# One bfloat16 matmul with two columns for the sum of squares of each weight unit, in place of two float32 matmuls

## The chip, the core and the metric

The kernel runs on one core of one Trainium2 chip. The metric is the device time of one execution in microseconds (us). The program is built with a scheduler that sets the order of the instructions on every engine, so a small edit can move instructions far away from it.

## What is computed

Attention for 4 batches of 12 heads (448 tokens, head dimension 64, RMS-normalized q and k), and then two feed-forward layers on its output:

```python
scores = scale * np.matmul(q_n, k_n.transpose(0, 1, 3, 2))
attn = softmax(scores)
x = np.matmul(attn, v), heads merged        # 1792 x 768
g = x @ w_gate                              # 768 x 1536
x = (g * sigmoid(g)) * (x @ w_val) @ w_out  # 1536 x 768
h = x @ w_in                                # 768 x 2048
out = (h * np.cos(h)) @ w2_out              # 2048 x 768
```

The weights arrive as 64-bit floats.

## The kernel before

Large products run on TensorE (PE) in float16 pairs: a weight and an activation are each split into a high and a low part, and three matmuls of 448 columns (lines 1002 to 1004 of `mm_piece`, line 1015 of `mm_out`) give the product. A weight must be scaled by a power of two before it is split, and this power comes from the sum of its squares.

Weights come in pieces of 128 partitions by 768 numbers. A piece goes through a chain: `load64` (DMA on the queue of SP into a tile `raw`, line 821; three such tiles in turn), `conv64` (three VectorE operations, lines 841 to 843, 64-bit to float32 in a tile `w`), `squares` (ScalarE Square with a running sum over the free axis, line 861; its full output lands in the upper half of the same `raw` tile, so that `raw` is free for the next load only after the Square), `unit_scale` (line 868: a matmul of a tile `full` of ones by the sums, which adds them over the 128 partitions and hands the total to every partition), `pow2_scale` (four small VectorE operations, lines 848 to 853: floor, exponent, the inverse scale `winv`, the scale `wsc`), `split16` (ScalarE high part, line 873; VectorE low part, line 874).

A unit is the set of pieces that share a scale: two pieces for each of 6 gate units, 6 val units and 8 units of `w2_in` (20 units), one piece for each of the 16 units of `w2_out`. There are 56 pieces and 36 units. `unit_scale` issues one float32 matmul of one column per piece and adds the two of a unit in PSUM:

```python
for i, n in enumerate(q):
    nc.tensor.matmul(ps[:, :1], full, n[:, 0:1], start=(i == 0), stop=(i == len(q) - 1))
```

Its output takes one of the three PSUM banks `s`, which the attention scores use too. The sums sit in tiles `nm` of a ring of 8, which other small results share.

The stages in time: from 0 to about 99 us the attention of the first batch is prepared and started (q and k are loaded, normalized and split, and turned by transposing DMAs on SP's queue, line 614; ScalarE copies what they bring, line 623, VectorE too, lines 621 and 622, and the scores follow, line 634). From 99 to about 335 the gate and val weights go through the chain (12 units of two) between the scores of the next batch (lines 444 and 453) and the first feed-forward products. From 335 to 737 the remaining batches run with weights that are ready. From 737 to 1106 the last batch and then the product with `w2_in` run; the 8 units of `w2_in` and the 16 of `w2_out` go through the chain meanwhile (`pre_step`, `w_conv`, `w_scale`), and `fin_h` (lines 1134 to 1149) computes the cosine. From 1106 on the product with `w2_out` runs alone.

SP issues the DMAs in its program order; a DMA that waits for a buffer holds back those behind it. The other engines also run their rows in order.

Of the kernel before, what the change touches and what calls it, by code (L numbers as in the profile page):

```python
# [9 lines left out]
F32 = mybir.dt.float32  # L10
F32R = mybir.dt.float32r
F16 = mybir.dt.float16
BF16 = mybir.dt.bfloat16
I32 = mybir.dt.int32
AF = mybir.ActivationFunctionType
ALU = mybir.AluOpType
# [124 lines left out]
def kernel(ctx: ExitStack, tc, q, k, v, g_q, g_k, w_gate, w_val, w_out, w2_in, w2_out, out):  # L141
    nc = tc.nc
    B, H, S, D = q.shape
    P = 128
# [12 lines left out]
    const = ctx.enter_context(tc.tile_pool(name="const", bufs=1))  # L157
# [15 lines left out]
    nm_p = ctx.enter_context(tc.tile_pool(name="nm", bufs=8))  # L173
# [16 lines left out]
    def bank(pool, tag):  # L190
        return pool.tile([P, 512], F32, tag=tag, name=tag)
# [8 lines left out]
    fold = const.tile([P, HP], F32, name="fold")  # L200
    ones = const.tile([P, P], F32, name="ones")
    full = const.tile([P, P], F32, name="full")
    NU = 36
    winv = const.tile([P, NU], F32, name="winv")
    wsc = const.tile([P, NU], F32, name="wsc")
    vsc = const.tile([P, 2 * B], F32, name="vsc")
# [11 lines left out]
    def emit_consts(gtmp):  # L218
        nc.sync.dma_start(gk, g_k.partition_broadcast(P))
        nc.sync.dma_start(gtmp, g_q.partition_broadcast(P))  # L220
        nc.vector.memset(half, -0.5)
        nc.vector.memset(hpi, math.pi / 2)
        make_identity(nc, ident)
        for h in range(2):
            hs = slice(HP * h, HP * h + HP)
            nc.gpsimd.tensor_copy(fold[hs], ident[hs, hs])
        nc.gpsimd.memset(full, 1.0)
        nc.gpsimd.tensor_copy(id16, ident)
        nc.gpsimd.memset(ones, 0.0)
        for h in range(2):  # L230
            hs = slice(HP * h, HP * h + HP)
            nc.gpsimd.memset(ones[hs, hs], 1.0)
# [583 lines left out]
    sq_dst = [None]  # L816
# [28 lines left out]

    def pow2_scale(ps, inv, sc):
        n = nm_p.tile([P, 4], F32, tag="nm", name="nm")
        nc.vector.tensor_scalar(n[:, 0:1], ps, 1e-30, None, op0=ALU.max)
        nc.vector.tensor_scalar(
            n[:, 1:2].bitcast(I32), n[:, 0:1].bitcast(I32), 1, 0x7F800000, op0=ALU.logical_shift_right, op1=ALU.bitwise_and  # L850
        )
        nc.vector.tensor_scalar(inv, n[:, 1:2], 2.0 ** 49, None, op0=ALU.mult)
        nc.vector.reciprocal(sc, inv)
# [3 lines left out]

    def squares(u, w32):
        q = nrm_t.setdefault(u, [])
        n = nm_p.tile([P, 4], F32, tag="nm", name="nm")  # L860
        nc.scalar.activation(sq_dst[0], w32, AF.Square, accum_out=n[:, 0:1])
        q.append(n)

    def unit_scale(u):
        q = nrm_t.pop(u)
        ps = bank(ps_s, "s")
        for i, n in enumerate(q):
            nc.tensor.matmul(ps[:, :1], full, n[:, 0:1], start=(i == 0), stop=(i == len(q) - 1))
        pow2_scale(ps[:, :1], winv[:, u:u + 1], wsc[:, u:u + 1])

    def split16(u, w32):
        wp = wp_tile(F16)
# [34 lines left out]
    def w_conv(j):  # L907
        if j >= len(pieces) or not pieces[j]["fresh"] or pieces[j]["kind"] == "out2":
            return
        pc = pieces[j]  # L910
        w32_t[j] = conv64(raw_t.pop(j))
        if pc["kind"] != "out1":
            squares(unit_of(pc), w32_t[j])

    def w_scale(j):
        if j < len(pieces) and pieces[j]["fresh"] and pieces[j]["last"] and pieces[j]["kind"] in ("gate", "val", "h"):
            unit_scale(unit_of(pieces[j]))
# [45 lines left out]
    def pre_step(more=True):  # L963
        done = False
        if pre_split and (pre_split[0][0] == "out2" or len(pre_split) > 1):
            kind, c, k0, w32 = pre_split.pop(0)
            if kind == "h":
                for kind, c, k0, w32 in ((kind, c, k0, w32), pre_split.pop(0)):
                    stores.append((scr[kind, c, k0], split16(UNIT0[kind] + c, w32)))
            done = True  # L970
        if pre_scale and (pre_scale[0][0] == "out2" or len(pre_scale) > 1):
            kind, c, k0, w32 = pre_scale.pop(0)
            unit_scale(UNIT0[kind] + c)
            if kind == "h":
                pre_split.append((kind, c, k0, w32))
                pre_split.append(pre_scale.pop(0))
            done = True
        if pre_conv:
            kind, c, k0, rw = pre_conv.pop(0)
            w32 = conv64(rw)  # L980
            squares(UNIT0[kind] + c, w32)
            if kind == "out2":
                stores.append((o32[c // 2][:, c % 2 * 768:(c % 2 + 1) * 768], w32))
            pre_scale.append((kind, c, k0, w32))
            done = True
        if pre_load and more:
            kind, c, k0 = pre_load.pop(0)
            rw = load64(w2_out, c, 0, 1, 768) if kind == "out2" else load64(w2_in, k0, c, 3, 256)
            pre_conv.append((kind, c, k0, rw))
            done = True  # L990
        return done
# [74 lines left out]
    def y_scale(b):  # L1066
        n = nm_p.tile([P, 4], F32, tag="nm", name="nm")
        nc.vector.tensor_reduce(n[:, 0:1], ynrm[:, b * KX:(b + 1) * KX], axis=AX.X, op=ALU.add)
        ps = bank(ps_s, "s")
        nc.tensor.matmul(ps[:, :1], full, n[:, 0:1], start=True, stop=True)  # L1070
        pow2_scale(ps[:, :1], ysc[:, B + b:B + b + 1], ysc[:, b:b + 1])
        ts = nc.vector.tensor_scalar
        sy, yi = ysc[:, b:b + 1], ysc[:, B + b:B + b + 1]
        ts(yhi[:, b, 0:1], yi, 1.0 / TWO_PI, None, op0=ALU.mult)
        ts(yhi[:, b, 1:2], yi, -1.0, None, op0=ALU.mult)
        ts(yhs[:, b, 0:1], sy, -PI_HI, None, op0=ALU.mult)
        ts(yhs[:, b, 1:2], sy, -PI_LO, None, op0=ALU.mult)
# [97 lines left out]
    c_p = start_ctx.enter_context(tc.tile_pool(name="cp", bufs=1))  # L1175
    gtmp = start_ctx.enter_context(tc.tile_pool(name="gtmp", bufs=1)).tile([P, D], F32, name="gtmp")
    emit_consts(gtmp)
    for i in range(3):
        c_const(i)
# [26 lines left out]
    for b in range(B):  # L1206
        sched = {}
        if b + 1 < B:
# [3 lines left out]
            for n in range(nst):  # L1212
                u = min(u for u in range(per) if sum(wt[:u + 1]) * nst > n * sum(wt))
# [52 lines left out]
    for c in range(NH):  # L1266
        j0 = j
        j += 2
        for b in range(B):
            ps = [bank(ps_s, "s"), bank(ps_t, "t")] if nh % 3 == 2 else [bank(ps_m, "mm") for _ in range(2)]  # L1270
# [28 lines left out]
    while j < len(pieces):  # L1299
        ps = [None] * nt  # L1300
# [49 lines left out]
```

## Time and profile before

| | |
|---|---|
| median of 3 runs | 1346.54 us (1341.5 to 1349.18) |
| profiled execution, first to last instruction | 1339.1 us |
| around that span in the runs | 2.4 us (fastest run) to 10.1 us (slowest), 7.4 at the median |
| PE busy | 1191.8 us (89%) |
| VectorE (DVE) busy | 880.0 us (66%) |
| ScalarE (ACT) busy | 681.0 us (51%) |
| GpSimd (POOL) busy | 471.9 us (35%) |

The profile shows the profiled execution by its span; its own time as a run is not listed apart, so the three runs' times stand beside it. Busy shares are means over stages with different limits. A wait row says who waited for whom, the total, the number of times and the longest. A timeline row gives start, duration and, in brackets, the idle time before it and what ended it; where rows overlap, the step from one start to the next is the cost.

### The profile page before, as it was taken

Reading aid. Unit: us, or ns where it says so; the run is one execution under the profiler, and the core shown is the slowest. Engines: PE = TensorE matmul, PEld = TensorE weight load, DVE = VectorE, ACT = ScalarE, POOL = GpSimd, SP = SyncE. Lnnn points to the kernel's source line nnn. Section 1 sums busy time; section 2 is a strip of 40 time slices with the busy share of each in tenths; the row PEclk is TensorE's granted clock in tenths of the full one; section 3 lists DMA queues with packets and bytes.
Section 4 is the critical chain, followed back from the end, with each engine's and each line's share of the span. In section 5 each row is a group of like instructions: output and inputs, shape, how many; then the busy total and the mean of one; then the engine's idle time right before and its main releaser. Section 6 shows DMA issues by size and latency. Waiting matters only on the chain.

```text
span 1339.1 us, 18253 instructions
## 1 busy us (share of the span) xinstructions
PE 1191.8 (89%) x6454; PEld 673.1 (50%) x6454; DVE 880.0 (66%) x1556; ACT 681.0 (51%) x1318; POOL 471.9 (35%) x351
## 2 busy tenths in 40 slices
PE   0688787778799988999899998999999998999998
PEld 0233243334674434864447654865555544666665
DVE  6878978999967788647773299668778886200000
ACT  2567577776435556445565266457777776100000
POOL 8621325555733456533545113413233232000000
PEclk9889798888889989999999999999999998999999
DMA  7535559987999987788867688650112237433221
GB/s 241 143 86 144 175 148 238 253 211 217 256 310 283 234 159 158 196 245 190 189 138 181 226 274 318 232 187 0 48 48 70 73 130 228 166 96 101 59 89 42
DMA packets 255196, 227.03 MB, mean 170 GB/s; under 512 B 177280, under 2 KB 205952, under 8 KB 255104
## 3 DMA queue, kind: packets, MB, share of 16 engines
q1 hardware_dynamic: 255104, 225.86, 60.0%
q8 instruction: 50, 0.82, 0.2%
q14 instruction: 42, 0.34, 0.1%
HBM read 147.13 MB, written 38.77 MB: 139 GB/s over the span
## 4 chain that ended last, share of the span: by engine, by line
PE 36%; DVE 19%; ACT 9%; DMA 8%; issue 5%; POOL 1%; SPq 1%; ACTq 0%; DVEq 0%; POOLq 0%
PE mm L1015 7%; PE s L1015 7%; PE mm L1002 6%; PE mm L1004 5%; PE mm L1003 5%; DMA PT<-p 3%; DMA T<-h 3%; DVE w L842 2%; PE t L1015 2%; ACT tmp L1143 2%; ACT tmp L1142 2%; DVE tmp L1140 2%; DVE tmp L1141 2%; DVE w L841 2%; DVE w L843 1%
## 5 line engine op out<-in xcount | busy, mean ns | idle before, releaser
L1002 PE MATMUL mm<-xy,wp 128*128 128x448 f16 x840 | 302.7, 361 | 22.8 <-ACT wp L873 8.9
L1003 PE MATMUL mm<-xy,wp 128*128 128x448 f16 x840 | 302.7, 360 | 0.0
L1004 PE MATMUL mm<-xy,wp 128*128 128x448 f16 x840 | 298.7, 360 | 2.6 <-DVE wp L874 2.4
L1015 PEld LDWEIGHTS <-g 128*128 128x128 f16 x1344 | 132.4, 98 | 92.8 <-issue 7.1
L1002 PEld LDWEIGHTS <-wp 128*128 128x128 f16 x960 | 96.8, 101 | 119.3 <-issue 22.7
L1004 PEld LDWEIGHTS <-wp 128*128 128x128 f16 x960 | 94.5, 99 | 97.4 <-issue 7.7
L1003 PEld LDWEIGHTS <-wp 128*128 128x128 f16 x960 | 95.6, 100 | 93.5 <-issue 16.0
L496 POOL TENSOR_TENSOR p<-pr,p 128x448 f16<-128x448 f32 x72 | 89.9, 1253 | 139.5 <-ACT p L487 120.9
L1149 POOL TENSOR_TENSOR g<-tmp,g 128x448 f16<-128x448 f32 x64 | 71.4, 1127 | 175.7 <-ACT g L1148 175.7
L943 POOL TENSOR_TENSOR wp<-w,wp 128x768 fp32r<-128x768 f32 x48 | 95.7, 1997 | 79.7 <-ACT wp L942 54.9
L463 ACT ACTIVATE pr<-s,sm,esc 128x448 f32<-128x448 f32 x126 | 90.1, 717 | 62.7 <-DVE sm L457 57.3
L1002 PE MATMUL mm<-g,wp 128*128 128x448 f32 x288 | 108.8, 378 | 0.1
L1003 PE MATMUL mm<-g,wp 128*128 128x448 f32 x288 | 107.6, 374 | 0.0
L1004 PE MATMUL mm<-g,wp 128*128 128x448 f32 x288 | 106.8, 371 | 0.1
L1015 PE MATMUL mm<-wp,g 128*128 128x384 f16 x576 | 101.0, 330 | 3.8 <-DVE tmp L1144 3.8
L1050 POOL TENSOR_TENSOR g<-tmp,g 128x448 fp32r<-128x448 f32 x48 | 63.1, 1329 | 106.2 <-ACT g L1049 106.0
L1015 PE MATMUL s<-wp,g 128*128 128x384 f16 x576 | 100.3, 328 | 0.0
L453 DVE TENSOR_REDUCE sm<-s 128x1 f32<-128x448 f32 x126 | 75.4, 615 | 19.7 <-PE s L444 19.5
L487 ACT ACTIVATE p<-pr 128x448 f16<-128x448 f32 x126 | 70.0, 571 | 30.6 <-DMA PT<-p 29.8
L321 POOL TENSOR_TENSOR ri<-ss,half 128x14 f32<-128x14 f32 x24 | 65.1, 2716 | 46.5 <-DVE ss L319 39.9
L841 DVE TENSOR_SCALAR w<-raw 128x768 int32<-128x768 int32 x68 | 49.6, 739 | 47.9 <-POOL wp L943 21.1
L842 DVE SCALAR_TENSOR_TENSOR w<-raw,w 128x768 int32<-128x768 int32 x68 | 80.2, 1190 | 0.7
(182 smaller groups left out, 2146.6 us busy)
## 6 DMA issues: line engine op xcount, KB each, us to landing
raw<-in_moe_w_out_dram SPq DMA_DIRECT2D x28, 768.0 KB, 5.4
wp<-scr_gate SPq DMA_DIRECT2D x36, 384.0 KB, 4.7
wp<-scr_val SPq DMA_DIRECT2D x36, 384.0 KB, 4.5
w<-scr_out SPq DMA_DIRECT2D x36, 384.0 KB, 4.3
raw<-in_moe_w_in_dram SPq DMA_DIRECT2D x16, 768.0 KB, 5.0
raw<-in_moe_w_gate_dram SPq DMA_DIRECT2D x12, 768.0 KB, 5.4
raw<-in_moe_w_val_dram SPq DMA_DIRECT2D x12, 768.0 KB, 4.6
wp<-scr_out SPq DMA_DIRECT2D x24, 384.0 KB, 3.0
```

The source lines that it names most:

```text
L453: nc.vector.tensor_reduce(sm[:, 0, t:t + 1], slot[n][:, :S], axis=AX.X, op=ALU.max)
L463: nc.scalar.activation(e, slot.pop(n)[:, :S], AF.Exp, bias=sm[:, 1, t:t + 1], scale=esc, accum_out=sm[:, 2, t:t + 1],)
L487: nc.scalar.activation(hi, slot[n], AF.Copy)
L496: eng.tensor_sub(p16[:, t - t0, 1], slot.pop(n), p16[:, t - t0, 0])
L841: nc.vector.tensor_scalar(wi, hi, 3, 0x3FFFFFF8, op0=ALU.logical_shift_left, op1=ALU.bitwise_and)
L842: nc.vector.scalar_tensor_tensor(wi, hi, -0x40000000, wi, op0=ALU.bitwise_and, op1=ALU.bitwise_or)
L943: nc.gpsimd.tensor_sub(wl, w32, wh.bitcast(F32))
L1002: nc.tensor.matmul(ps[f][:, :S], wh[:, s], x[:, 0], start=(first and i == 0), stop=False)
L1003: nc.tensor.matmul(ps[f][:, :S], wh[:, s], x[:, 1], start=False, stop=False)
L1004: nc.tensor.matmul(ps[f][:, :S], wl[:, s], x[:, 0], start=False, stop=(last and i == n - 1))
L1015: nc.tensor.matmul(ps[:, :CO], x[:, a, p0:p0 + P], rhs, start=st, stop=sp)
L1149: nc.gpsimd.tensor_sub(x[:, 1], r, x[:, 0])
```

## The change

The ones are also kept as a bfloat16 tile `full16`. The running sums of a unit's pieces go to columns 0 and 1 of one tile `nu` (a ring of 6 of its own). One bfloat16 matmul takes the upper 16 bits of these float32 sums (a view with a step of two elements) as its two columns, or its one column for a unit of one piece. The two totals are then added on VectorE by one operation more. Line numbers after the edit are 2 to 8 higher.

```diff
+    full16 = const.tile([P, P], BF16, name="full16")
...
+        nc.gpsimd.memset(full16, 1.0)
...
     def pow2_scale(ps, inv, sc):
         n = nm_p.tile([P, 4], F32, tag="nm", name="nm")
-        nc.vector.tensor_scalar(n[:, 0:1], ps, 1e-30, None, op0=ALU.max)
+        if ps.shape[1] == 2:
+            nc.vector.tensor_scalar(n[:, 2:3], ps[:, 0:1], 1e-30, None, op0=ALU.max)
+            nc.vector.tensor_tensor(n[:, 0:1], ps[:, 1:2], n[:, 2:3], op=ALU.add)
+        else:
+            nc.vector.tensor_scalar(n[:, 0:1], ps, 1e-30, None, op0=ALU.max)
...
     def squares(u, w32):
         q = nrm_t.setdefault(u, [])
-        n = nm_p.tile([P, 4], F32, tag="nm", name="nm")
-        nc.scalar.activation(sq_dst[0], w32, AF.Square, accum_out=n[:, 0:1])
+        if not q:
+            q.append(nm_p.tile([P, 4], F32, tag="nu", name="nu", bufs=6))
+        n = q[0]
+        nc.scalar.activation(sq_dst[0], w32, AF.Square, accum_out=n[:, len(q) - 1:len(q)])
         q.append(n)
 
     def unit_scale(u):
         q = nrm_t.pop(u)
+        m = len(q) - 1
         ps = bank(ps_s, "s")
-        for i, n in enumerate(q):
-            nc.tensor.matmul(ps[:, :1], full, n[:, 0:1], start=(i == 0), stop=(i == len(q) - 1))
-        pow2_scale(ps[:, :1], winv[:, u:u + 1], wsc[:, u:u + 1])
+        nc.tensor.matmul(ps[:, :m], full16, q[0].bitcast(BF16)[:, 1:2 * m:2], start=True, stop=True)
+        pow2_scale(ps[:, :m], winv[:, u:u + 1], wsc[:, u:u + 1])
```

The scheduler places other instructions differently too. Three places follow.

**Start, queues of SP and ACT.** SP's queue before, from the load of the second gate piece on (`raw<-` loads a weight piece, `T<-h` is the transposing DMA of one pair of heads; what a row waits for is in brackets):

```order
L821 DMA raw<-in_moe_w_gate_dram 128x3x512 [waits DMAHW7_49,DMAHW5_49,DVE_49]
L821 DMA raw<-in_moe_w_val_dram 128x3x512 [waits DMAHW6_49,DMAHW0_49,DVE_49]
L614 DMA_TRANSPOSE T<-h_313 128x14x128 [waits Pool_49]
L281 DMA rqk<-in_k_dram 64x448
L281 DMA rqk<-in_k_dram 64x448 [waits DMAHW1_49]
L284 DMA rqk<-in_q_dram 128x448 [waits DMAHW2_49]
L614 DMA_TRANSPOSE T<-h_335 128x14x128 [waits DMAHW3_49,Pool_49]
```

SP's queue after the change, from the same load on:

```order
L823 DMA raw<-in_moe_w_gate_dram 128x3x512 [waits DMAHW7_49,DMAHW5_49,DVE_49]
L823 DMA raw<-in_moe_w_val_dram 128x3x512 [waits DMAHW6_49,DMAHW0_49,DVE_49]
L823 DMA raw<-in_moe_w_val_dram 128x3x512 [waits DMAHW1_49,Activation_49]
L616 DMA_TRANSPOSE T<-h_315 128x14x128 [waits Pool_49]
L283 DMA rqk<-in_k_dram 64x448
L283 DMA rqk<-in_k_dram 64x448 [waits DMAHW2_49]
L286 DMA rqk<-in_q_dram 128x448 [waits DMAHW3_49]
L616 DMA_TRANSPOSE T<-h_337 128x14x128 [waits DMAHW4_49,Pool_49]
```

ACT's queue at the same place before (`h` is the split q and k of a pair of heads, `cC` a copy of what its transposing DMA brought):

```order
L392 ACTIVATE h_313<-rqk 128x7x64
L392 ACTIVATE h_335<-rqk 128x7x64
L623 ACTIVATE cC<-T 64x896
L378 ACTIVATE h_384<-rqk 128x7x64
L392 ACTIVATE h_384<-rqk 128x7x64
```

and after the change:

```order
L394 ACTIVATE h_315<-rqk 128x7x64
L394 ACTIVATE h_337<-rqk 128x7x64
L869 ACTIVATE raw,nu<-w_738 128x768
L869 ACTIVATE raw,nu<-w_813 128x768
L869 ACTIVATE raw,nu<-w_887 128x768
L625 ACTIVATE cC<-T 64x896
L380 ACTIVATE h_386<-rqk 128x7x64
L394 ACTIVATE h_386<-rqk 128x7x64
```

The Squares of the first three pieces (line 869, 861 before) now stand ahead of the copy that waits for the first transposing DMA, and the load of the fourth piece, which waits for ACT (its `raw` tile is the first piece's), stands ahead of that DMA on SP.

**DVE, a val unit of two pieces in the stretch from 99 to 335 us.** Before, from the end of the conversion of the unit's second piece (`w_1782`) to the four small operations:

```order
L843 SCALAR_TENSOR_TENSOR w_1782<-raw,w_1782 128x768
L398 TENSOR_TENSOR h_2250<-rqk,h_2250 128x7x64
L843 SCALAR_TENSOR_TENSOR w_1858<-raw,w_1858 128x768
L384 TENSOR_TENSOR h_2250<-rqk,h_2250 128x7x64
L453 TENSOR_REDUCE sm<-s 128x1 x2
L848 TENSOR_SCALAR nm<-s 128x1
L849 TENSOR_SCALAR nm<-nm 128x1
L852 TENSOR_SCALAR winv<-nm 128x1
L853 RECIPROCAL wsc<-winv 128x1
L874 SCALAR_TENSOR_TENSOR wp<-w_1718,wsc,wp 128x768
```

and after the change, the same unit (`w_1779`):

```order
L845 SCALAR_TENSOR_TENSOR w_1779<-raw,w_1779 128x768
L845 SCALAR_TENSOR_TENSOR w_1854<-raw,w_1854 128x768
L851 TENSOR_SCALAR nm<-s 128x1
L1043 TENSOR_SCALAR nm<-winv,vsc 128x1
L852 TENSOR_TENSOR nm<-s,nm 128x1
L455 TENSOR_REDUCE sm<-s 128x1
L855 TENSOR_SCALAR nm<-nm 128x1
L455 TENSOR_REDUCE sm<-s 128x1
L1047 SCALAR_TENSOR_TENSOR tmp<-tmp,mm 128x448
L858 TENSOR_SCALAR winv<-nm 128x1
L455 TENSOR_REDUCE sm<-s 128x1
L1047 SCALAR_TENSOR_TENSOR tmp<-tmp,mm 128x448
```

One conversion of the next piece is all that now stands between the end of the unit's conversion and the first operation on its total (`L851`). The small operations, which stood together right ahead of the low part (line 874), now have maxima of scores and products of the gate between them; the reciprocal (line 859) is the next row.

**ACT, last units of one piece (`w2_out`), around 1065 to 1080 us.** Before, with the Squares of `w_10300` and `w_10377` behind the high parts (line 873) of the units before:

```order
L873 ACTIVATE wp<-w_10076,wsc 128x768
L873 ACTIVATE wp<-w_10126,wsc 128x768
L1143 ACTIVATE tmp<-tmp,hpi,ht 128x448
L1148 ACTIVATE g_10263<-tmp 128x448
L1134 ACTIVATE tmp<-mm,ht 128x448 x2
L861 ACTIVATE raw,nm<-w_10300 128x768
L1148 ACTIVATE g_10272<-tmp 128x448
L1142 ACTIVATE tmp<-tmp 128x448 x2
L1143 ACTIVATE tmp<-tmp,hpi,ht 128x448 x2
L1134 ACTIVATE tmp<-s,ht 128x448
L1134 ACTIVATE tmp<-t,ht 128x448
L861 ACTIVATE raw,nm<-w_10377 128x768
```

and after the change, where `w_10359` is the piece that was `w_10377`, and `w_10059`, `w_10109` are those that were `w_10076`, `w_10126`:

```order
L1142 ACTIVATE tmp<-mm,ht 128x448
L869 ACTIVATE raw,nu<-w_10359 128x768
L1156 ACTIVATE g_9972<-tmp 128x448
L1150 ACTIVATE tmp<-tmp 128x448
L1151 ACTIVATE tmp<-tmp,hpi,ht 128x448
L1150 ACTIVATE tmp<-tmp 128x448
L1151 ACTIVATE tmp<-tmp,hpi,ht 128x448
L881 ACTIVATE wp<-w_10059,wsc 128x768
L881 ACTIVATE wp<-w_10109,wsc 128x768
```

The Square of that piece moved from eleven rows behind the first of these high parts to six rows ahead of it. Those of its three neighbours moved likewise, while their matmuls on PE stand behind the same count of products as before.

## Rows read from the trace of the kernel before

**Rows 1.** Stretches of the span; columns: us, busy time of each engine (instructions), PEclk, DMA share, GB/s.

```profile
0.00:99.00 99.00, 48.68 (x189) 17.84 (x190) 76.16 (x141) 44.75 (x77) 58.61 (x59) 0.91 0.57 158
99.00:335.00 236.00, 185.29 (x914) 85.03 (x914) 206.00 (x330) 163.16 (x334) 99.67 (x69) 0.88 0.72 197
...
737.00:892.00 155.00, 150.60 (x795) 103.45 (x794) 105.91 (x205) 71.80 (x124) 43.26 (x26) 1.00 0.76 260
892.00:1106.00 214.00, 210.99 (x1127) 110.23 (x1126) 176.74 (x348) 160.41 (x281) 63.30 (x58) 1.00 0.19 62
```

**Rows 2.** PE timeline; start us, duration us, line, op, operands, xcount, then idle before it.

```profile
946.63 0.35 PE L1004 MATMUL t<-xy,wp 128*128 128x448 f16 x1
946.82 0.50 PE L868 MATMUL s<-nm,full 128*128 128x1 f32 x4
947.18 0.35 PE L1002 MATMUL mm<-xy,wp 128*128 128x448 f16 x1
```

**Rows 3.** PE timeline around a unit of one piece.

```profile
806.58 0.28 PE L868 MATMUL s<-nm,full 128*128 128x1 f32 x2
806.75 0.35 PE L1002 MATMUL mm<-xy,wp 128*128 128x448 f16 x1
```

**Rows 4.** Weight loads and matmuls of line 868 over the span; duration min/median/max.

```profile
L868 PEld LDWEIGHTS s<-nm,full x112: 186/190/338, 99.5 to 1096.4; 128*128 128x128 f32 x112
L868 PE MATMUL s<-nm,full x112: 165/250/373, 99.5 to 1096.5; 128*128 128x1 f32 x112
```

**Rows 5.** Weight loads of float16, from the costliest groups; xcount | busy us, mean ns.

```profile
L1002 PEld LDWEIGHTS <-wp 128*128 128x128 f16 x960 | 96.8, 101 | 119.3 <-issue 22.7
```

**Rows 6.** Waits of PE from 892 to 1106; us in total, times, longest.

```profile
PE s L868 <- ACT raw L861: 2.7, 3, 1.2
```

**Rows 7.** Waits of PE from 1106 on.

```profile
PE mm L1015 <- DVE tmp L1144: 3.8, 1, 3.8
```

**Rows 8.** Timeline of all engines where one unit of two pieces is finished.

```profile
312.11 1.81 DVE L843 SCALAR_TENSOR_TENSOR w<-raw,w 128x768 int32<-128x768 int32 x2
313.09 0.84 ACT L861 ACTIVATE raw<-w 128x768 f32<-128x768 f32 x1 [3.42 <-DVE w L843]
313.84 0.19 ACT L861 ACTIVATION_READ_ACCUMULATOR raw<-w 128x1 f32 x1
...
314.08 0.38 PE L868 MATMUL s<-nm,full 128*128 128x1 f32 x2 [2.29 <-ACT raw L861]
```

**Rows 9.** DVE timeline of small operations.

```profile
181.66 0.15 DVE L849 TENSOR_SCALAR nm<-nm 128x1 int32<-128x1 int32 x1
181.85 0.16 DVE L852 TENSOR_SCALAR winv<-nm 128x1 f32<-128x1 f32 x1
```

**Rows 10.** Waits of DVE from 99 to 335.

```profile
DVE wp L874 <- ACT wp L873: 7.4, 6, 2.0
...
DVE nm L848 <- PE s L868: 3.4, 2, 2.6
```

**Rows 11.** Waits of PE from 99 to 335.

```profile
PE s L868 <- ACT raw L861: 10.6, 4, 4.1
```

**Rows 12.** Timeline of the SP queue at the start.

```profile
28.29 2.58 SPq L614 DMA_TRANSPOSE T<-h  x1
...
57.20 0.38 SPq L821 DMA_DIRECT2D raw<-in_moe_w_val_dram  x1
```

**Rows 13.** Timeline of ACT at the start.

```profile
24.65 0.58 ACT L392 ACTIVATE h<-rqk 128x448 f16<-128x448 f32 x1 [1.31 <-POOL rqk L364]
33.73 0.95 ACT L623 ACTIVATE cC<-T 64x896 f16<-64x896 f16 x1 [8.50 <-DMA T<-h]
...
56.23 0.85 ACT L861 ACTIVATE raw<-w 128x768 f32<-128x768 f32 x1
```

**Rows 14.** Timeline of DVE at the start.

```profile
29.11 1.67 DVE L843 SCALAR_TENSOR_TENSOR w<-raw,w 128x768 int32<-128x768 int32 x1
...
34.73 0.39 DVE L621 COPY cB<-T 64x896 f16<-64x896 f16 x1
```

## The prediction

> **What bounds the kernel now.** I read the stretches of the span first, then the waits of the engine that is short in each, then single places in the timeline. From 737 us on PE is the bound: it is busy 150.6 of 155 us up to 892 and 211.0 of 214 up to 1106, at the full clock [rows 1]. What PE saves there shortens the run. From 99 to 335 no engine is full, but DVE is nearest, with 206 of 236 us busy against 185 for PE [rows 1]; an operation more on DVE counts nearly in full there, and matmul time counts little. Up to 99 us PE is busy half of the time [rows 1]: a chain of loads, splits and transposing DMAs sets the pace, and a delay in it delays all that follows.
>
> **What a unit costs on PE.** A float32 matmul of line 868 leaves two weight loads and two matmuls in the trace: 112 of each for 56 pieces, a load taking 190 ns [rows 4]. A unit of two pieces holds the stream for 947.18 - 946.82 = 0.36 us, where a product of 448 columns takes 0.19 [rows 2]. A unit of one piece holds it for 806.75 - 806.58 = 0.17 us [rows 3]. After the change a unit is one weight load and one matmul of one or two columns. No row shows a bfloat16 matmul so narrow. Its bounds are half of the one-piece unit, since half of the passes are left, 0.08 us, and a whole product of 448 columns, 0.19 us. I take 0.10, because such a short matmul should cost about its weight load, and 16-bit loads take 101 ns [rows 5]. That saves 0.26 us per unit of two pieces and 0.07 per unit of one.
>
> The Trainium skill ("FP8 and Floating Point Precision", section "TensorE Precision Notes") says that true FP32 takes four passes through the array. The trace shows two loads and two matmuls per operation, not four. By the rule a single pass would be 0.17/4 = 0.04 us, an estimate from that page, and the 24 units after 737 us would save some 1.4 us more than my sum has.
>
> **Part 1, from 737 us on.** There are 8 units of two pieces (of `w2_in`) and 16 of one (of `w2_out`): 8 x 0.26 + 16 x 0.07 = 3.2 us saved, all on the bound engine. With the two bounds of a unit this is between 1.0 and 4.1 us.
>
> PE also waits there for the Square of a piece: 2.7 us in three waits [rows 6]. The order after the change puts the last Squares of `w2_out` from eleven rows behind two high parts to six rows ahead of them, and leaves the matmuls at the same place in PE's stream. A row of ACT of 448 columns takes 0.58 us [rows 13], so the Squares come several us earlier than the matmuls need them, and I take all 2.7 as saved (none, if DVE's conversions ahead of the Squares are late instead). DVE, busy 177 of 214 us [rows 1], has room for one small operation more per unit, which costs nothing there; without that room the five units of two in this stretch would cost 1 us. Sum of part 1: 5.9 us saved, between 1.0 and 6.8. What follows at once is the product with `w2_out`; its first matmul that waits does so for the cosine chain on DVE, 3.8 us [rows 7]. That chain starts from PE's last products, so I let it move along with them.
>
> **Part 2, from 99 to 335 us.** Twelve units of two pieces pass here. Each has one DVE operation more. Small ones follow each other at 181.85 - 181.66 = 0.19 us [rows 9], so 12 x 0.19 = 2.3 us; DVE is busy 87% there, and I count 2.0 (bounds 0 and 2.3).
>
> The order changes more than that. The way from the end of a conversion through Square, its accumulator read and the matmul to the total is 314.08 + 0.38 - 313.09 = 1.4 us with nothing in the way [rows 8]. Before, in the unit shown, a conversion, two splits and two maxima of scores stood over it on DVE; after the change four val units have one conversion alone, 1.81/2 = 0.9 us [rows 8]. DVE then waits 0.5 us in each, 1.9 in all (0 if ACT and PE run ahead, 5.6 if no row covers it). PE's 10.6 us of waits for Squares [rows 11] remain in some form and are not on the bound.
>
> In return rows now stand between the reciprocal and the low part in units where none stood. DVE lost 7.4 us in six such waits for the high part, and 3.4 for totals [rows 10]. I count 4 of the 7.4 as recovered (0 to 7.4), since three of the twelve units had no cover before and every unit has some now. Part 2 is thus 2.0 + 1.9 - 4 = 0, with bounds of 7.4 saved and 7.9 lost.
>
> **Part 3, the start.** The load of the fourth weight piece needs the `raw` tile of the first, which its Square releases. Before, that Square ran at 56.23 [rows 13], and the load followed at 57.20, long after the first transposing DMA, issued at 28.29 [rows 12]. Now the load stands ahead of that DMA on SP, and SP must wait for the Square. The Square was moved up as well, but it cannot start before its conversion ends, 29.11 + 1.67 = 30.78 [rows 14]; ACT is free then, its row before ends at 25.23 [rows 13]. It takes 1.0 us [rows 8], and the issue of the load 0.38 [rows 12], so that the transposing DMA is issued at about 32.3, 4.0 us later. Queued behind it on SP are the loads of q and k of the next pairs and the second and third transposing DMAs. ACT's copy, at 33.73 before [rows 13], waits for what it brings, and with it the split of the third pair, which stands behind that copy; so the third is late by 4 too. DVE's copy at 34.73 [rows 14] slips to about 37.7, but a conversion of 0.9 us that stood behind it is done ahead now, so DVE waits from about 35.6 and loses some 2.0. Between 2.0 and 4.0 I take 3.0, because up to 99 us latency counts more than any engine's work; the lower end is 0, if slack behind it takes all. The new memset on POOL is one of several small ones ahead of work that waits for loads, and costs nothing; without that cover it is a fraction of a microsecond.
>
> **Sum.** 3.0 + 0 - 5.9 = 2.9 us saved against the span of 1339.1 us, so 1336.2. The median of the runs is 7.4 us above this span, so the time is 1343.6 us. That is 0.2% below the median; 0.5% (6.7 us) is about what a measurement of this kernel can tell from no change.
>
> **The rivals.** *A, the new order is better than its parts.* After the change the units of the second stretch come evenly, three scores apart. If DVE loses neither the 7.4 nor the 3.4 us [rows 10] and meets no new wait, and the start's slip is absorbed, the time is 1346.5 - 5.9 - 10.8 + 2.0 = 1331.8. For it: no unit is left without cover ahead of its low part. Against it: four units have less cover ahead of the total than any before.
>
> *B, SP's queue, the other side.* A load of weights that waits for a Square ahead of a transposing DMA costs 4.0 us at the start, and from about the fifteenth load on most loads stand one to three transposing DMAs earlier than before. Each that meets a late Square stops SP, and behind it the DMAs that feed the scores. With 5.9 us saved it takes 12.6 us, so the fourth such stop makes the run slower by over 0.5%; four give 1346.5 - 5.9 + 16 = 1356.6. For it: DMAs of the attention end waits of ACT in every stage. Against it: the Squares moved up too, and most loads are issued long before they are needed.
>
> *C, the saving is not passed on.* If the cosine chain [rows 7] does not move along, what PE saves after 892 us only lengthens its wait of 3.8, and about 1.6 us from before 892 is left: 1346.5 - 1.6 + 3.0 = 1347.9.
>
> *D, the change does not do what it says.* If the narrow matmul costs 0.19 us, the gain of 3.2 falls to 1.0 and the time is 1345.8.
>
> **How the numbers follow.** My forecast, with D beside it, 0.34, and C 0.10 lie within 0.5% (1339.8 to 1353.3): 0.44 for the same. A has 0.32, since the lost DVE and PE waits in the second stretch are larger than any cost that I can name. B has 0.24. The range reaches from A with the better bound of part 1 (1331.8 less 0.9, and 2 more should it also end some of PE's waits [rows 11]) to just past B: 1329 to 1358. It leaves out a fifth: the far ends of A and B.
>
> **What would show it.** Right: 36 weight loads in `unit_scale` instead of 112, near 100 ns each; steps near 0.1 us at the units after 737; no wait of PE for Squares from 892 to 1106; the first transposing DMA issued near 32.3; DVE waiting for the total in the val units. Wrong: that DMA still at 28; waits of DVE for high parts as long as before; the stretch from 99 to 335 shorter or longer by over 8 us; or a wait at the first products with `w2_out` that has grown by what PE saved.

## The result, and the profile after

The changed kernel takes 1357.88 us (median of 6 runs, 1352.97 to 1362.59) against 1344.72 for the kernel before in the same session: ratio 1.0099, 95% interval 1.0075 to 1.0122. It is slower by 1%, where 1343.6 was forecast. The time is inside the range, but the change was forecast to save 2.9 us and costs some 13.

First what was priced. PE's timeline at a unit of two pieces, which answers to [rows 2], and at a unit of one:

```profile
974.66 0.35 PE L1012 MATMUL t<-xy,wp 128*128 128x448 f16 x1
974.85 0.17 PE L876 MATMUL s<-nu,full 128*128 128x2 bf16 x1
974.88 0.35 PE L1010 MATMUL mm<-xy,wp 128*128 128x448 f16 x1
...
1090.75 0.17 PE L876 MATMUL s<-nu,full 128*128 128x1 bf16 x1
1090.78 0.35 PE L1010 MATMUL s<-xy,wp 128*128 128x448 f16 x1
```

The next product starts 0.03 us behind the sum in both, where it was 0.36 for two pieces and 0.17 for one. I had taken 0.10. The Trainium skill ("FP8 and Floating Point Precision", section "TensorE Precision Notes") has true FP32 take four passes; the estimate of 0.04 for a single pass that I worked out from that is nearer here than the 0.10 that I took from rows. The four passes themselves show in no run here. Line 876 over the span, for [rows 4], has 36 of each, a load of about 98 ns:

```profile
L876 PEld LDWEIGHTS <-full x36: 95/98/98, 98.2 to 1123.4; 128*128 128x128 bf16 x36
L876 PE MATMUL s<-nu,full x36: 163/167/178, 98.2 to 1123.6; 128*128 128x2 bf16 x20, 128*128 128x1 bf16 x16
```

SP's queue at the start, for [rows 12]: the first transposing DMA is issued at 32.36, where 32.3 was forecast. But by 98 us the slip is gone: the first sum of a unit runs at 98.2, where it ran at 99.5 [rows 4]. The traces of the experiments below say more: where the order of the start is the changed one, that sum runs at 95.5 to 97.8 (11 traces), and where it is that of before, at 100.5 to 102.2 (6). So by then the changed start is some 4 us ahead, not 3 behind.

```profile
26.11 6.19 SPq L823 DMA_DIRECT2D raw<-in_moe_w_val_dram  x2
32.36 2.83 SPq L616 DMA_TRANSPOSE T<-h  x1
```

Waits of DVE (first two) and of PE (last two) from 99 to 335 us, for [rows 10] and [rows 11]: DVE's wait for the high part fell from 7.4 to 3.2 us and its wait for totals from 3.4 to 2.3, as forecast, but PE waits 26.0 us for high parts, where it waited 8.9 before (second fence). Its wait for exponentials, 12.9 us before, is 0.9 now.

```profile
DVE wp L882 <- ACT wp L881: 3.2, 3, 1.5
DVE nm L851 <- PE s L876: 2.3, 4, 1.2
...
PE mm L1010 <- ACT wp L881: 26.0, 7, 7.3
PE s L876 <- ACT raw L869: 9.9, 6, 4.3
```

```profile
PE s L444 <- ACT pr L463: 12.9, 8, 4.6
...
PE mm L1002 <- ACT wp L873: 8.9, 6, 2.7
```

No engine is full there, and the stretch as a whole lost or gained little: its last unit's sum runs at 314.90 (PE's timeline), before at 314.08 [rows 8].

```profile
314.90 0.16 PE L876 MATMUL s<-nu,full 128*128 128x2 bf16 x1 [4.27 <-ACT raw L869]
```

From the first unit's sum to the last it takes 216.7 us, before 214.6; the other traces spread from 215 to 218 in the order of before and from 213 to 218 in the changed one, so no difference shows.

Laying PE's matmuls of the two traces side by side (by their count, the sums of the units left out), the changed kernel is 0 us behind at 413 us, 9 behind at 450, 14 at 700, 28 at 918, and 22 at the end. Of these 22 only 13 lie between the medians: the changed kernel's profiled execution was the longest of its six runs (1362.59), and the one before, with a span of 1339.1 us, is at the short end of its runs, so what is read off this pair can be too large by up to 9 us. Still, the time goes where the edited instructions are few or none, from 413 to 700, most of it by 450, and in the stretch before 918. That stretch by windows, for [rows 1] (busy time and instructions of PE, weight loads, DVE, ACT, POOL, then granted clock, DMA share, GB/s): the changed kernel, begun at 751 since it is 14 us behind there, then the kernel before:

```profile
751.00:919.00 168.00, 152.60 (x776) 100.80 (x775) 108.25 (x210) 72.28 (x127) 44.61 (x26) 0.97 0.73 246
```

```profile
737.00:905.00 168.00, 163.60 (x863) 110.17 (x862) 118.78 (x232) 81.61 (x137) 43.26 (x26) 1.00 0.72 246
```

In the same 168 us PE does 11 us less than before, DVE 11 and ACT 9; the DMAs move as much. So the three engines have come to wait, and PE is no longer full where my sum had it full. Its granted clock, 0.97 against 1.00, has dropped too.

The end of y at 905 to 918 is the largest single step. Timelines of ACT, DVE and PE of the changed kernel:

```profile
910.87 0.84 ACT L869 ACTIVATE raw<-w 128x768 f32<-128x768 f32 x1 [4.81 <-DVE winv L858]
914.68 0.84 ACT L869 ACTIVATE raw<-w 128x768 f32<-128x768 f32 x1 [2.87 <-DVE nm L855]
915.52 0.52 ACT L1065 ACTIVATE tmp<-mm 128x448 f32<-128x448 f32 x1
...
908.24 0.56 DVE L843 TENSOR_SCALAR w<-raw 128x768 int32<-128x768 int32 x1 [3.20 <-DMA raw<-in_moe_w_in_dram]
912.05 0.56 DVE L843 TENSOR_SCALAR w<-raw 128x768 int32<-128x768 int32 x1 [1.00 <-DMA raw<-in_moe_w_in_dram]
917.60 0.16 DVE L1076 TENSOR_REDUCE nm<-ynrm 128x1 f32<-128x6 f32 x1 [2.55 <-ACT mm L1066]
...
917.81 0.37 PE L1078 MATMUL s<-nm,full 128*128 128x1 f32 x1 [5.24 <-DVE nm L1076]
```

The last evictions of y (line 1065) stand on ACT behind Squares of `w2_in` pieces (line 869), those behind conversions on DVE (line 843), and those behind loads that have not landed. `y_scale` (line 1076) comes last, and PE waits 5.24 us for it. In the kernel before, only the first of these two conversions stands ahead of that reduction (line 1068), the second stands behind it, and PE does not wait:

```profile
887.98 0.57 DVE L841 TENSOR_SCALAR w<-raw 128x768 int32<-128x768 int32 x1 [2.10 <-DMA raw<-in_moe_w_in_dram]
...
890.71 0.14 DVE L1068 TENSOR_REDUCE nm<-ynrm 128x1 f32<-128x6 f32 x1
...
897.21 0.56 DVE L841 TENSOR_SCALAR w<-raw 128x768 int32<-128x768 int32 x1
```

### The profile page after: what moved, and what is told of

Read it like the earlier page. It is cut to its first block, busy times and chain, and to the rows that moved or that the text cites. A ratio compares the mean times of both kernels' runs of the same rounds, so it can differ in the third digit from the quotient of the medians.

```text
span 1360.8 us, 18117 instructions
## 1 busy us (share of the span) xinstructions
PE 1187.6 (87%) x6378; PEld 661.5 (49%) x6378; DVE 877.6 (64%) x1576; ACT 680.6 (50%) x1318; POOL 481.9 (35%) x352
## 4 chain that ended last, share of the span: by engine, by line
PE 35%; DVE 11%; DMA 7%; ACT 6%; issue 3%; POOL 1%; SPq 1%; ACTq 0%; DVEq 0%; POOLq 0%
PE mm L1023 7%; PE s L1023 6%; PE mm L1010 5%; PE mm L1011 5%; PE mm L1012 5%; PE t L1023 2%; DMA T<-h 2%; DVE w L844 2%; DMA PT<-p 1%; PE t L557 1%; ACT tmp L1150 1%; DVE tmp L1148 1%; DVE tmp L1149 1%; ACT tmp L1151 1%; DVE w L845 1%
## 5 line engine op out<-in xcount | busy, mean ns | idle before, releaser
L1157 POOL TENSOR_TENSOR g<-tmp,g 128x448 f16<-128x448 f32 x64 | 71.7, 1133 | 177.8 <-ACT g L1156 177.7
L1058 POOL TENSOR_TENSOR g<-tmp,g 128x448 fp32r<-128x448 f32 x48 | 67.0, 1411 | 121.5 <-ACT g L1057 121.2
L869 ACT ACTIVATE raw<-w 128x768 f32<-128x768 f32 x56 | 47.0, 839 | 75.7 <-DVE w L845 60.7
L1168 ACT ACTIVATE tmp<-mm,osc 128x384 f32<-128x384 f32 x8 | 4.6, 580 | 148.6 <-PE mm L1023 147.8
```

The source lines that it names most:

```text
L1058: nc.gpsimd.tensor_sub(x[:, 1], a, x[:, 0].bitcast(F32))
L1157: nc.gpsimd.tensor_sub(x[:, 1], r, x[:, 0])
```

## The experiments

The program's order is the scheduler's. To tell an instruction's price from that of the order, one file holds both forms of the sum and takes three switches: the tiles come from the ring of their own (`nu`), the sum goes by bfloat16 (`bf`), one matmul of two columns with the add (`two`). Before is (0, 0, 0), the change (1, 1, 1). It builds the program `ORDER_OF`, notes each engine's order, and builds `RUN` with every instruction tied, for issue only, to the one that the noted order has ahead of it on its engine. The sums of the units are left untied, the added operation stands behind the one it follows in the code.

```diff
+                for k in order[eng]:
+                    chain += [kept[k]] + behind.get(kept[k].name, [])
+                for x, y in zip(chain, chain[1:]):
+                    tc.add_manual_dep(y, x.name, info, reason="order")
```

`CUTS` changes to another order from a place on PE on (1020 runs at about 337 us, 3057 at 737, 3900 at 905), `ON` limits this to some engines, `MOVES` puts instructions behind another one. Theory O: the order costs the time. Its rivals are named in the texts. All ratios are to the kernel before, measured beside each run, 5 rounds each; a row with the sum "as changed" has the changed kernel's instructions.

| run | sum | order | median us | ratio | interval |
|---|---|---|---|---|---|
| e17 | two float32 | before | 1344.15 | 1.0000 | 0.9985 to 1.0016 |
| e1 | two bfloat16 | before | 1347.96 | 1.0027 | 1.0013 to 1.0040 |
| e12 | two bfloat16 | its own | 1345.13 | 0.9989 | 0.9974 to 1.0004 |
| e3 | two bfloat16 | changed | 1355.80 | 1.0080 | 1.0061 to 1.0100 |
| e2 | two float32 | changed | 1354.87 | 1.0070 | 1.0048 to 1.0092 |
| e4 | one float32 | changed | 1356.53 | 1.0078 | 1.0058 to 1.0098 |
| e5 | two bfloat16 | before; changed 337 to 737 | 1352.88 | 1.0062 | 1.0042 to 1.0083 |
| e6 | two bfloat16 | before; changed 737 to 905 | 1359.82 | 1.0112 | 1.0086 to 1.0139 |
| e7 | two bfloat16 | changed; before 337 to 905 | 1345.13 | 0.9999 | 0.9988 to 1.0011 |
| e13 | as changed | changed; before 737 to 905 | 1348.35 | 1.0031 | 1.0017 to 1.0045 |
| e14 | as changed | changed; before from 337 | 1348.37 | 1.0029 | 1.0014 to 1.0044 |
| e15 | two bfloat16 | before; ACT, DVE changed 737 to 905 | 1359.17 | 1.0105 | 1.0086 to 1.0125 |
| e18 | two bfloat16 | before; DVE changed 737 to 905 | 1360.42 | 1.0103 | 1.0078 to 1.0128 |
| e16 | two bfloat16 | changed; SP before 737 to 905 | 1355.23 | 1.0084 | 1.0056 to 1.0111 |
| e8 | as changed | changed, end of y moved | 1356.95 | 1.0092 | 1.0072 to 1.0111 |
| e9 | as changed | the same, Squares later | 1357.43 | 1.0079 | 1.0062 to 1.0096 |
| e10 | as changed | changed, one DMA moved | 1358.70 | 1.0088 | 1.0067 to 1.0108 |
| e11 | as changed | e9 and e10 | 1361.16 | 1.0115 | 1.0095 to 1.0135 |

### Instructions or order

e1, e2, e3, e4 (the settings alone, written shorter than in the files, here and below):

```diff
+ORDER_OF, RUN = (0, 0, 0), (1, 1, 0)   # e1
+ORDER_OF, RUN = (1, 1, 1), (1, 0, 0)   # e2
+ORDER_OF, RUN = (1, 1, 1), (1, 1, 0)   # e3
+ORDER_OF, RUN = (1, 1, 1), (1, 0, 1)   # e4
```

> The sums go by bfloat16 (two accumulating matmuls of one column each, no add), and every engine issues in the order that the kernel before has. Theory O (the order that the scheduler chose for the changed kernel costs the time, the new instructions save a little): the saving alone is left, 2 to 6 us, ratio 0.996 to 0.999. Rival B (the bfloat16 matmul itself, with its every-other-element column, costs the time): about 1.010. Rival W (the single matmul, which has to wait for both Squares, costs the time): 0.996 to 0.999 as well, since the pair is kept here.

> The sums are the two float32 matmuls of the kernel before, no add, and every engine issues in the order that the changed kernel has. Theory O: as slow as the changed kernel or 2 to 5 us slower, ratio 1.008 to 1.014. Rivals B and W: the instructions that cost the time are not there, 0.998 to 1.003.

> The same instructions as in the first of these kernels (two bfloat16 matmuls of one column, no add), in the changed kernel's order. Theory O: 1.007 to 1.012, though not one instruction differs from the first kernel. Rival B: 1.010 here and there. Rival W: 0.996 to 0.999 here and there.

> The changed kernel with its one matmul of two columns in float32, in the changed kernel's order. Theory O: the changed kernel's time or up to 3 us more, 1.008 to 1.013. Rival B: 0.998 to 1.003. Rival W: 1.008 to 1.013.

Three kinds of sum in the changed order, two of them in float32, take 1.0070 to 1.0080; their intervals reach into that of the changed kernel. (O's ranges for e2 and e4 began at 1.008, so both lie just under them.) The old instructions in the new order are slow (e2), so B and W cannot carry the loss. e1 and e3 have the same instructions, and the order alone is worth 1355.8 - 1348.0 = 7.8 us. What e1 was to save is not there: it is 0.27% (some 3.6 us) over before, the wrong side of what O said. e12 is again the pair of bfloat16 matmuls, in the order that the scheduler gives them by itself. Its edit against the kernel before, shortened (`m` is the number of the unit's pieces):

```diff
-        n = nm_p.tile([P, 4], F32, tag="nm", name="nm")
-        nc.scalar.activation(sq_dst[0], w32, AF.Square, accum_out=n[:, 0:1])
+        if not q:
+            q.append(nm_p.tile([P, 4], F32, tag="nu", name="nu", bufs=6))
+        n = q[0]
+        nc.scalar.activation(sq_dst[0], w32, AF.Square, accum_out=n[:, len(q) - 1:len(q)])
...
-        for i, n in enumerate(q):
-            nc.tensor.matmul(ps[:, :1], full, n[:, 0:1], start=(i == 0), stop=(i == len(q) - 1))
+        for i in range(m):
+            nc.tensor.matmul(ps[:, :1], full16, q[0].bitcast(BF16)[:, 2 * i + 1:2 * i + 2], start=(i == 0), stop=(i == m - 1))
```

> The instructions of the first and the third experiment (two bfloat16 matmuls of one column, no add), in the order that the scheduler gives them by itself, which is neither that of before nor that of the changed kernel. Theory O (every such edit draws a new order, and the draw is worth more than the edit): anywhere from 0.995 to 1.012, apart from 1.0027 by more than the intervals. Rival W (only the form with a single matmul gets a slow order): 0.998 to 1.003.

One set of instructions thus ran at 0.9989, 1.0027 and 1.0080 in three orders, and its own order is a good one. That lies in what both O and W allowed, so it doesn't tell them apart; as a price of the instruction W falls by e2, and by e13 and e14 below. Whether a unit in one matmul draws slow orders more often than one in two wasn't tried. e17 has the float32 sums in the old order, on the new tiles:

```diff
+ORDER_OF, RUN = (0, 0, 0), (1, 0, 0)   # e17
```

> Every instruction and the order of every engine as in the kernel before (two float32 matmuls, no add; one of the 20 sums stands one place away on TensorE); only the tiles that take the sums of the Squares come from the ring of their own that the change made. What the first experiment and the last but two have over before, 0.3 per cent, is either this ring and where things lie in memory (theory R: 1.002 to 1.004 here) or the bfloat16 matmuls themselves (theory B: 0.999 to 1.001 here).

It shows too that tying the order of before costs nothing by itself. It clears the ring of tiles, and points to the bfloat16 sums for the 0.27% of e1; the two intervals (to 1.0016, from 1.0013) just overlap, so that is not shown, and the same bfloat16 pair is level with the kernel before in e12 and in e7 below.

### Which stretch

```diff
+CUTS = ((1020, (1, 1, 1)), (3057, (0, 0, 0)))   # e5, ORDER_OF (0, 0, 0)
+CUTS = ((3057, (1, 1, 1)), (3900, (0, 0, 0)))   # e6, ORDER_OF (0, 0, 0)
+CUTS = ((1020, (0, 0, 0)), (3900, (1, 1, 1)))   # e7, ORDER_OF (1, 1, 1); RUN (1, 1, 0) in all three
+CUTS = ((3057, (0, 0, 0)), (3900, (1, 1, 1)))   # e13, RUN (1, 1, 1)
+CUTS = ((1020, (0, 0, 0)),)                     # e14, RUN (1, 1, 1)
```

> The instructions of the first experiment (two bfloat16 matmuls of one column). All engines issue in the order of the kernel before up to the matmul that runs at about 337 us, in the changed kernel's order to the one at about 737 us, and in the order of before from there. Theory O, by places (the traces of the two orders, with the same instructions, part by 4 to 6 us in this stretch, nearly all of it at 430 to 450 us): 4 to 6 us over the first experiment, ratio 1.005 to 1.008. Rival S (an order is worth what it is as a whole; a piece of it alone costs nothing): 1.002 to 1.003, as the first experiment.

> As the one before it, with the changed kernel's order only from about 737 us to just behind the last scale of y, about 905 us. Theory O, by places (the two orders part by 11 to 12 us here, most of it at 880 to 918 us): 1.009 to 1.012. Rival S: 1.002 to 1.003.

> The complement: the changed kernel's order up to about 337 us and from about 905 us on, where its trace runs 7 us and 4 us shorter than the order of before, and the order of before between them. Theory O, by places: 8 to 11 us less than the first experiment, ratio 0.994 to 0.997, which is faster than both kernels. Rival S: 1.002 to 1.008.

> The changed kernel, all its instructions and its order, but from about 737 us to just behind the last scale of y (about 905 us) every engine issues in the order of before. Theory O, by places (11 to 12 us of the loss lie in this stretch): ratio 0.998 to 1.002, no slower than before. Rival S (an order is worth what it is as a whole): 1.008 to 1.010.

> The changed kernel, all its instructions, in its own order up to about 337 us and in the order of before from there to the end. Theory O, by places: the 4 to 5 us of the stretch from 337 to 737 us go too, the 4 us that the changed order gains at 1100 us are lost: 0.997 to 1.002. Rival W (the single matmul with its wait for both Squares, and the add, cost time by themselves): 1.005 or more.

e5 and e6 came where O put them: over e1, by the ratios, the order of 337 to 737 costs 4.7 us and that of 737 to 905 costs 11.4. e7 gained 3.8 us on e1, not 8 to 11: of that forecast, 7 us up to 337 had been read off one profiled execution of e1 that was the longest of its 12 runs (1351.93, 4 us above their median). e13 and e14 give the changed kernel itself, no instruction of it altered, the old order in the stretch or from 337 us on, and it is at 1.003. That is above O's ranges, which ended at 1.002, and below the 1.005 that W gave for e14. So about 0.7 of the changed kernel's 1% is the order from 737 to 905. The last 0.3% is e1's; the single matmul and the add (e13, e14) cost no more than the pair (e1).

### Which engine

```diff
+ON = ("Activation", "DVE")   # e15, CUTS of e6
+ON = ("DVE",)                # e18, CUTS of e6
+ON = ("SP",)                 # e16, CUTS of e13, RUN (1, 1, 0)
```

> The instructions and the order of the first experiment (two bfloat16 matmuls, order of before), but from about 737 to 905 us ScalarE and VectorE alone issue in the changed kernel's order; TensorE, GpSimd and SyncE keep that of before. Theory A (in the changed order the Squares of later weight pieces stand up to 12 places further ahead on ScalarE and hold up what is behind them): 1.009 to 1.012, the whole of what the stretch costs. Rival Q (it is the order of the loads on SyncE's queue): 1.002 to 1.004, as the first experiment.

> The instructions and the order of the third experiment (two bfloat16 matmuls, changed kernel's order), but from about 737 to 905 us SyncE alone issues its DMAs in the order of before (34 lines of difference: one load of a w_in piece stands 18 places further back, three other loads 3 or 4). Theory A: 1.007 to 1.009, as the third experiment. Rival Q: 0.998 to 1.001.

> The first experiment (two bfloat16 matmuls, order of before), but from about 737 to 905 us VectorE alone issues in the changed kernel's order. Theory A (ScalarE, whose Squares stand ahead of evictions, carries the loss): 1.002 to 1.005, as the first experiment. Rival V (VectorE's conversions of pieces that have not landed, ahead of the scale of y, carry it): 1.008 to 1.012.

The order of DVE alone carries the cost of the stretch (10.2 us over e1 by the ratio, 11.4 with all engines in e6); ACT's adds none that shows to it (e15), and SP's put back takes none away (e16), so theory A falls as it was put. Of DVE's 1556 rows only a few dozen stand elsewhere, and the end of y tells what some of them do. DVE's timeline in e18, and PE's wait from 737 to 912 us:

```profile
902.01 0.57 DVE L849 TENSOR_SCALAR w<-raw 128x768 int32<-128x768 int32 x1 [3.13 <-ACT mm L1088]
...
908.25 0.56 DVE L849 TENSOR_SCALAR w<-raw 128x768 int32<-128x768 int32 x1 [3.42 <-DMA raw<-in_moe_w_in_dram]
...
911.17 0.14 DVE L1098 TENSOR_REDUCE nm<-ynrm 128x1 f32<-128x6 f32 x1
...
PE s L1100 <- DVE nm L1098: 5.6, 1, 5.6
```

ACT's evictions of y are done at 902 here, but the reduction of `y_scale` (line 1098) stands behind two conversions (line 849), the second of which waits 3.42 us for its load. In e1, the same program but for DVE's order in this stretch, that conversion stands between two low parts of y (line 1122), its load is there, and PE waits for nothing of y:

```profile
900.69 0.14 DVE L1098 TENSOR_REDUCE nm<-ynrm 128x1 f32<-128x6 f32 x1
...
904.43 3.88 DVE L1122 SCALAR_TENSOR_TENSOR xy<-tmp,ysc,xy 128x448 f16<-128x448 f32 x4
908.22 0.55 DVE L849 TENSOR_SCALAR w<-raw 128x768 int32<-128x768 int32 x1
```

Of the 11 us by which these two traces part in the stretch, 8 lie at 895 to 905. Windows of that place, e1's and then e18's, begun 3 us later since it is 3 us behind there, and a part of the second:

```profile
895.00:912.00 17.00, 17.00 (x92) 9.57 (x91) 12.33 (x34) 11.81 (x20) 0.00 (x0) 1.00 0.57 199
```

```profile
911.20:916.00 4.80, 4.64 (x14) 2.16 (x15) 3.92 (x19) 3.25 (x4) 0.00 (x0) 0.53 0.00 0
898.00:915.00 17.00, 11.41 (x52) 6.34 (x51) 9.43 (x32) 6.08 (x13) 0.00 (x0) 0.82 0.64 208
```

The wait is 5.6 of the 8. Behind it PE runs near the lower of its two clock levels (1.2 and 2.4 GHz): 0.53 granted from 911.2 to 916.0, where e1 has 1.00. An estimate from that is 4.8 x 0.47 = 2.3 us more, so a wait of the bound engine cost more than its own length here.

The other traces bear the pattern out. In all nine that have DVE's changed order in this stretch (the changed kernel, e2, e3, e4, e6, e10, e15, e16, e18), 56 of DVE's 68 conversions stand ahead of y's last reduction, and PE waits 3.9 to 8.7 us for y's scale. In all seven that have the order of before there (before, e1, e5, e7, e13, e14, e17) it is 55, and PE does not wait. e12, with its own order, also has 56, but its last conversion waits only 1.27 us for its load, PE waits 1.5 us, and the run is level with before. That this one row makes the whole 10 us is not shown: no run moves it alone in e18.

### Moving what waits

e8 and e9 move the Squares and conversions of the end of y, e10 moves the transposing DMA that blocks SP at 422 us, e11 does e9 and e10 (the moves in words, in the files they are numbers of instructions):

```diff
+MOVES = (ACT: Square of piece 1 behind y's last eviction, of pieces 2 and 3 behind the last split of y;
+         DVE: conversions of pieces 2 and 3 behind the last split of y)                # e8
+MOVES = (the same, pieces 2 and 3 behind the first 16 steps of h)                      # e9
+MOVES = (SP: transposing DMA into T behind the next two of p, the store of sums, the loads of R)   # e10
```

> The changed kernel and its order, with one thing moved: the first three Squares of the later w_in pieces (and the conversions of the second and third piece) are issued behind the last four evictions of y and the scale of y (the second and third behind the split of y), not ahead of them. Theory Y (ScalarE and VectorE stand in front of weight pieces that have not landed while y's end waits behind them): 6 to 10 us less than the changed kernel, ratio 1.001 to 1.005. Rival N (the pieces come late for the h stage then, so the wait only moves): 1.008 to 1.010, as the changed kernel.

> As the experiment before (the changed kernel with the end of y ahead of the Squares of the later w_in pieces), but the second and third of those Squares and their conversions now stand behind the first 16 steps of h, since there they made the evictions of h wait (5.64 us at 925 us). Theory Y2: the 5 to 7 us of the wait for y's scale are gone and nothing comes in their place, 1.000 to 1.005. Rival L (the whole of w_out and w_in weight work runs late in this order, so the next wait takes the time): 1.008 to 1.010.

> The changed kernel and its order, with one DMA moved on SyncE's queue: the transposing DMA of the next pair's rows into T, which at 422 us waits 8.8 us for its buffer while two transposing DMAs of p stand behind it, is issued behind those two, the store of the sums and the loads of R. Theory T: the 5.9 us that TensorE waits for PT at 437 us go, 1.003 to 1.006. Rival N (TensorE then waits for the rows in T, or for the evictions of val, which are 3.9 us late right behind it): 1.008 to 1.010.

> Both moves together. If both waits are where the time went: 0.994 to 1.001, with the changed kernel's instructions. If neither: 1.008 to 1.010.

All four gain nothing. The rivals in the texts hold, N in e8 and e10 and (at 1.0079 for 1.008) L in e9: the move took its wait away and got another. Waits of PE in e8 from 895 to 1000, in e9 from 895 to 1133, and in e10 from 430 to 450 us:

```profile
PE mm L1032 <- DVE tmp L1174: 5.6, 1, 5.6
```

```profile
PE mm L1032 <- DVE tmp L1174: 9.0, 8, 2.2
```

```profile
PE s L452 <- ACT pr L471: 6.8, 2, 6.1
PE mm L1032 <- DVE tmp L1069: 4.2, 1, 4.2
```

In e8 PE now waits for the first evictions of h (line 1174), 5.6 us for 5.2. In e9 the conversions are made up during h, where DVE is busy 178 of 214 us, and PE waits 9 us in eight pieces. In e10 the wait for PT, 5.9 us in the changed kernel, became one for the exponentials (6.8). So the trace named the waits, but taking one away by hand did not bring the time back: of the runs of the changed kernel only those with the old order of the stretch (e13, e14) did.

## Why the prediction was wrong

- **The unit's price.** Right in kind, missed in size on the safe side: 0.03 us held on PE, not 0.10. With the measured steps the 3.2 us of part 1 would have been 8 x 0.33 + 16 x 0.14 = 4.9. (The upper bound of 4.1 did not follow from its 0.08: that gives 8 x 0.28 + 16 x 0.09 = 3.7.) Rival D is out.
- **The start.** The event hit to 0.1 us, but the cost of 3.0 had the wrong sign: by the first unit's sum the changed order is some 4 us ahead, outside my bounds of 0 to 4.0 lost. What gains them was not looked for, and by 413 us the changed kernel is only level with the one before.
- **Part 2.** Net 0 forecast, and no difference shows over the traces; DVE's waits for high parts and totals shrank as said. PE's wait of 26.0 us for high parts, which I had not seen, did not lengthen the stretch.
- **Part 1.** In the changed kernel's trace the waits for Squares from 919 us on are gone, as forecast, and the wait at the first `w2_out` product is 1.3 us, where it was 3.8 [rows 7]; from 918 to the end it makes up 6 us. But only 1 of the 6 is made up during h, where PE now waits 3.7 us for DVE (line 1152), the other 5 at the first products with `w2_out`. And both belong to the new order. In the old one (waits of PE from 880 to 1150 us, e1 below) the Squares still cost 2.4 us, where e17 has 2.7, and the wait at the first `w2_out` product is 5.2, where e17 has 3.8. So in this pair of traces rival C's mechanism is what shows: the cosine chain doesn't move along, and the wait grows by part of what PE saved.

```profile
PE mm L1045 <- DVE tmp L1174: 5.2, 1, 5.2
PE s L895 <- ACT raw L878: 2.4, 3, 1.5
```

- **The step that failed is the sum itself.** It priced the edited instructions and the order at three places, and between them let the old profile stand: no term for rows that change places from 335 to 737, and from 737 on PE stayed full, with what it saves shortening the run and DVE having room. Just there the new order costs 11.4 us (e6; 10.2 with DVE's alone, e18), and PE waits 3.9 to 8.7 us for y's scale, where it had not waited. The order of 337 to 737 costs another 4.7 (e5). None of the four signs of being wrong that I had listed showed, since all four watch places that I had priced.
- **Rival B** had the sign and nearly the time (1356.6), which is luck: its mechanism is not what shows. SP's loads of weights wait 208 us for Squares (38 waits) in the changed kernel, 214 (35) before. The stop of 8.8 us at 422 is a transposing DMA that waits for its own buffer, and it doesn't decide: e10 and e16 change SP's order and gain nothing.
- **The saving.** The 3 to 5 us of PE's time (forecast and by the measured steps) don't reach the end of the run in the old order: e1 is 3.6 us slower than before, e17 equal to it. One candidate is the clock. The mean granted clock of e1's 12 runs is 0.955, that of e17's 0.959, and among the runs of the kernel before 0.01 goes with 3 to 5 us; that would be 1 to 2 us of the 3.6. It is argued, not shown, since a lower clock can also follow from waits, as in e18; the rest is open.

Also open: why the order of 337 to 737 costs its 4.7 us, since the one wait tried there (e10) gave nothing, and why the scheduler placed the conversion where it did. The pieces don't add up exactly: the gaps of e5, e6 and e7 to e1, put on e1, would give e3 1.012, and it is at 1.0080. Likewise e13 keeps the changed order from 337 to 737 and e14 does not, and both are at 1.003. No version beats the kernel before by more than the measurement tells; e12 (0.9989) and e7 (0.9999) are level with it.

## What to carry to other kernels

Where a scheduler sets the order, a small edit draws a new order for the whole program, and the draw (here 0.9989 to 1.0080 for one set of instructions) can be worth more than the edit. So compare the order on every engine over the whole program, also on one that isn't full (DVE was busy 119 of 168 us from 737 to 905), and look for a row that waits for a load and has moved ahead of a row that the bound engine waits for. To judge the edit itself, run it in the old order; one wait moved by hand only showed the next one here.

## What the runs showed that I had not expected

- A bfloat16 sum of one or two columns holds PE's stream for 0.03 us (974.85 to 974.88, 1090.75 to 1090.78), a tenth of the float32 pair's 0.36.
- The order of DVE alone, busy about 70% of that stretch, costs some 10 us. The row that the traces point to is a conversion that waits 3.42 us for its load ahead of y's scale; PE then waits 5.6 us and runs on at 0.53 of its clock.
- One profiled execution can mislead about the place of a loss: e1's was 4 us above its median, and most of e7's expectation rested on it. The trace that shows the changed kernel was its longest run as well.
